# Loads of K and V in two row groups, and fewer stores in the last unit of an attention and mixer kernel

## The chip, the cores and the metric

The kernel runs on one core of a Trainium2 chip. The metric is the device time of one launch in microseconds (us). Five engines work side by side, each through its own queue in order: TensorE (PE: matmuls and transposes), VectorE (DVE), ScalarE (ACT), GpSimd (POOL) and SyncE (SP). Transfers between HBM and the on-chip memory run on 16 DMA engines. An engine issues a transfer as an instruction in its own queue; the data move later, and a semaphore tells of the landing.

## What is computed

Attention with pooled keys and values for 8 batches, 8 heads, 576 rows and 64 columns a head, then a token mixer and a channel mixer:

```python
k_p = k.reshape(B, H, Sp, 8, D).mean(axis=3)       # Sp = 576 / 8 = 72 pooled rows
v_p = v.reshape(B, H, Sp, 8, D).mean(axis=3)
scores = scale * np.matmul(q, k_p.transpose(0, 1, 3, 2))
attn = softmax(scores)                             # over the 72 pooled keys
x = heads_side_by_side(np.matmul(attn, v_p))       # 8 x 576 x 512
h = np.maximum(x.transpose(0, 2, 1) @ w_tok1, 0) @ w_tok2
u = x + h.transpose(0, 2, 1)
out = u + np.maximum(u @ w_ch1, 0) @ w_ch2         # w_ch1 512 x 1536
```

## The kernel before

Everything is one launch on one core, with the order of the work written out by hand: each engine executes its instructions in the order in which the program names them.

**Units.** The channel mixer is done in nine units. Units 0 to 7 are batches 0 to 7 with 512 of their 576 rows; unit 8 holds the last 64 rows of all batches together (the tails). A unit multiplies `u` with `w_ch1` on PE (L473), applies ReLU on ACT (L477) and multiplies with `w_ch2` (L496 in unit 0, L545 from unit 1 on, where the product is computed with sums of operands that VectorE prepares, L514 to L534).

**Schedule tables.** A unit is a generator with some 48 stops. At each stop, tables (L23 to L39) name the attention and token steps of later batches that are put in there. `K0`, `K1`, `V0`, `V1` pool half the heads of a batch's keys or values on POOL (L170, L171, L174 or L176), `k1` and `v1` the same on VectorE. `kpT` transposes the pooled keys on PE (L219) and copies them on VectorE (L221). `Q0`, `Q1` transpose queries on VectorE (L268), `s0` to `s3` are scores (PE L279, exponentials on ACT L285), `av` is the product with the values (PE L317, division on VectorE L335), `at`, `u` and `t` the token mixer (L363, L378, L388). `lk`, `lq`, `lv` issue the loads of a later batch's K, Q and V. A prefix gives the batch: `<` this unit's own, none the next, `>` the one after. `g` is a gate: VectorE sets a flag (L630) and POOL copies it (L631), so that POOL's next instructions start no earlier than that point of VectorE's order.

**Loads.** All loads of K, Q, V and weights are issued by POOL, since they cast from float32 to bfloat16. K and V of a batch are 72 pooled rows on 72 partitions, 8 heads and 8 rows of 64 each. Batch 0's are loaded in three parts (64 rows of four heads, the last 8 rows of all heads, 64 rows of the other four heads), those of batches 1 to 7 in one transfer of 576 KB. Each of the tiles `kr`, `vr` and `qb` has two buffers. Ahead of unit 0, POOL's order is (L660 to L682): K, Q, V of batch 0 (transfers 1 to 7), token weights (8 to 12), first channel weights (13 to 15), K of batch 1, a permutation of weights, Q and V of batch 1, second channel weights in three, then K and Q of batch 2. In unit 0 the step `lv2` stands at stop 10 and `K0` of batch 1 at stop 15, so POOL issues the load of batch 2's V ahead of that pooling; `lk3` at stop 16 and `V0` at 18 follow.

**Swap.** From batch 4 on, `u` is written to HBM (`mem`, L397) and read back in blocks (`v<-mem`, L404), both issued by SP, and transposed in blocks by VectorE (L411) into what the next unit's PE work reads.

**Stores.** A unit's output goes out from tiles of 128 partitions: two tiles of two 128-row groups (`oa` and `ob`, 512 columns each). `store` (L480) issues two transfers a tile from SP, one for each half of 64 partitions, because a group of 128 partitions holds rows of two kinds. In unit 8 the groups are the tails of two batches each; `oa` goes out with `store`, and `ob` in eight transfers (L572 to L581): for each column half, each of the two groups and each half of the partitions one, alternately on SP and ACT, as soon as the addition for that group is done.

Of the kernel before, what the change touches and what calls it, by code (L numbers as in the profile page):

```python
# [19 lines left out]

HEAD = """c0 c1 d8 q0 d1 q1 d5 kp0 kp1 kt0 d2 o0 e0 kt1 kp2 kp3 o1 e1 kt2 kt3 q2 q3 d2 o2 e2 vpool0 o3 d1 vpool1 e3 d2
          aw1 av0 av2 d2 av3 at_0 at_2 av4 at_1 at_3 d2 at_4 X0 X1 X2 A0 A1 A2 X3 A3 d3"""
FIRST = {0: "<u0", 2: "<u3", 6: "k1", 10: "lv2", 15: "K0 Q0", 16: "kpT Q1 lk3", 18: "V0 s1 <u2", 20: "s0",  # L23
         22: "lq3 v1 s2", 24: ">K0 s3", 25: "av1", 26: "av4", 27: "<u1 av3 av2", 30: ">K1", 32: "av0", 36: "at0 at1",
         38: "u3 >V0", 40: "u4 u0", 44: "lv3 u2 u1", 45: "t3 t0", 46: "t1", 47: "t2 t4"}
SECOND = {4: "g0", 7: ">K0 kpT", 8: "Q1", 9: "Q0", 11: "s2", 12: ">Q0", 13: ">Q1", 14: "v1 =3a s0", 15: "lv3 lk3",
          16: "s1", 17: "=1a", 18: "s3 =3b", 19: "av1", 20: "av3", 21: "av2", 22: "lq3", 23: ">K1 av0", 24: "av4",
          26: "g1", 27: "=1b", 28: ">kpT =2a", 29: "at0", 30: ">s3", 31: "=2b", 32: "=4b at1 =4a", 34: ">s2",
          36: "u2", 38: ">V0", 39: "u0 >s1 u3", 40: "t2", 41: "u1 t3", 42: ">s0 >V1 t0 t1"}
THIRD = {0: ">K0 av4 lk3 lq3", 2: "av3", 4: ">K1", 6: "av0", 9: "av2", 10: ">V0 av1", 12: "=3b", 14: "at0 at1",  # L30
         15: "=3a", 16: ">kpT", 17: "g0", 18: ">Q0", 19: "=1a u3 >s1", 20: ">Q1", 23: "u1 >s3 =2a", 24: "u0 =1b u2",
         25: "=2b t1", 26: ">s0", 28: "u4 >s2 =4b", 29: ">V1", 30: "=4a g1", 33: "t0", 34: "t2 >av3", 35: "t3",
         37: ">av4", 39: "t4 >av1", 41: "lv3", 42: ">av2", 44: ">av0"}
LATER = {0: ">Q0", 6: "=3a >K0", 7: "at0 at1", 8: ">K1 >kpT", 9: ">V0 u1 u0 >Q1", 10: "u3 >s1", 11: ">V1 u4",
         12: "u2", 13: ">s0", 14: "M0", 15: "M4 M2", 16: "M", 17: ">s3 lk3", 18: "=3b", 20: "=1a", 21: "g0",
         22: ">av3 =2a", 23: "=1b", 24: "lq3", 25: "=2b", 27: ">s2 =4a", 28: "=4b", 31: "g1 >av2", 36: ">av4",
         38: "T1 T3", 39: "T2", 40: "T0", 43: ">av0", 44: ">av1 lv3 T4"}
LAST = {14: "=3b", 22: "=1a", 24: "=2a =1b", 25: "=4a", 28: "=2b", 31: "=4b", 34: "=3a"}
PLANS = {0: FIRST, 1: SECOND, 2: THIRD, 8: LAST}  # L39


@with_exitstack
def kernel(
# [14 lines left out]
    nc = tc.nc  # L58
    B, H, S, D = q.shape
# [54 lines left out]
    def load_kv(b, src, key):  # L114
        t = loaded[b, key] = raw.tile([SP, H, POOL, D], BF16, name=key + "r")
        if b == 0:
            for h0, h1, j0, j1 in ((0, HP, 0, BP), (0, H, BP, SP), (HP, H, 0, BP)):
                kv(t, src, b, h0, h1, j0, j1)
        else:
            kv(t, src, b, 0, H)  # L120

    def load_q(b):
        qb = loaded[b, "q"] = raw.tile([P, HP, BR * D + D], BF16, name="qb")
# [9 lines left out]
    def load(key, b):  # L133
        if b < B:
            load_q(b) if key == "q" else load_kv(b, k if key == "k" else v, key)
# [334 lines left out]
    def l1_tile(n, m, uT):  # L470
# [6 lines left out]
        nc.scalar.activation(out=GT[:, m, :], in_=ps, func=AF.Relu)  # L477
        yield

    def store(n, g, o):  # L480
        for half in range(2):
            rows = slice(half * BP, (half + 1) * BP)
            if n == B:
                dst = out.rearrange("(c h) (p r) n -> h p c r n", h=2, r=BR)[half][:, 2 * g:2 * g + 2, 8, :]
            else:
                dst = out[n].rearrange("(p r) n -> p r n", r=BR)[:, 4 * g + half:4 * g + half + 3:2, :]
            nc.sync.dma_start(out=dst, in_=o[rows])

    def unit_plain(n, u):
# [46 lines left out]
    def unit_fast(n, u):  # L536
        last = n == B
        uT = moving(u)
        for m in range(NM):
            yield from l1_tile(n, m, uT)  # L540

        def product(ps, a, w, start, after, split=False):
            for i in range(2):
                for m in range(NH):
                    nc.tensor.matmul(out=ps[i] if split else ps[:, i], lhsT=a(m)[:, i * P:(i + 1) * P], rhs=w(m),  # L545
                                     start=start and m == 0 and (i == 0 or split), stop=(m == NH - 1),
                                     skip_group_check=True)
                    if (i * NH + m) % 4 == 3 and (i, m) != (1, NH - 1):
                        yield
                if split:  # L550
                    after(i)
            if not split:
                after(slice(0, 2))
            yield

        def bank(split=False):
            if split:
                return [ps_two.tile([P, 2, 512], FP32, name="p2")[:, 0, 0:256] for _ in range(2)]
            return ps_one.tile([P, 2, 256], FP32, name="p1")

        def keep(name):
            return outp.tile([P, 2, 256], FP32, name=name, bufs=1)

        def plus(out, ps, other, then=None):
            def go(i):
                nc.vector.tensor_tensor(out=out[:, i], in0=ps[i] if type(ps) is list else ps[:, i], in1=other[:, i],  # L566
                                        op=ALU.add)
                if then is not None:
                    then(i)
            return go  # L570

        def store_part(cols):  # L572
            def go(i):
                if not last:
                    return
                c = 2 + i
                for half in range(2):
                    (nc.scalar if half else nc.sync).dma_start(
                        out=out[2 * c + half].rearrange("(p r) n -> p r n", r=BR)[:, 8, cols],
                        in_=ob[half * BP:(half + 1) * BP, i, cols])  # L580
            return go  # L581

        SG, TW = fast["S"], fast["T"]
        u1, u2 = u["u"][:, 0:2], u["u"][:, 2:4]
        oa, ob = (outp.tile([P, 2, DM], FP32, name="o") for _ in range(2))
        x, y = bank(last), bank()
        s1 = keep("s1")
        yield from product(x, lambda m: GT[:, m, lo], lambda m: w_ch2[:, m, lo], True,
                           plus(s1, x, u1[:, :, lo]), last)
        yield from product(y, lambda m: GT[:, NH + m, lo], lambda m: w_ch2[:, NH + m, lo], True, plus(oa[:, :, lo], y, s1))  # L590
        z = bank()
        s5 = keep("s5")
        yield from product(z, lambda m: SG[:, 0, m], lambda m: TW[:, 0, m], True, plus(s5, z, u2[:, :, hi]))
        s2 = keep("s1")
        yield from product(x, lambda m: SG[:, 1, m], lambda m: TW[:, 1, m], False,
                           plus(s2, x, u1[:, :, hi]), last)
        if not last:
            w = bank()
            s4 = keep("s4")
            yield from product(w, lambda m: GT[:, NH + m, hi], lambda m: TW[:, 3, m], True, plus(s4, w, u2[:, :, lo]))  # L600
        yield from product(z, lambda m: SG[:, 3, m], lambda m: w_ch2[:, NH + m, hi], False, plus(oa[:, :, hi], z, s2))
        store(n, 0, oa)
        if last:
            yield from product(x, lambda m: SG[:, 2, m], lambda m: TW[:, 2, m], False,
                               plus(ob[:, :, hi], x, s5, store_part(hi)), True)
            yield from product(x, lambda m: GT[:, NH + m, hi], lambda m: TW[:, 3, m], False,
                               plus(ob[:, :, lo], x, u2[:, :, lo], store_part(lo)), True)
        else:
            def finish(i):
                plus(ob[:, :, hi], x, s5)(i)  # L610
                plus(ob[:, :, lo], x, s4)(i)
            yield from product(x, lambda m: SG[:, 2, m], lambda m: TW[:, 2, m], False, finish)
            store(n, 1, ob)
# [19 lines left out]
    def unit(n, at):  # L633
# [8 lines left out]
        for i, _ in enumerate((unit_fast if n >= 1 else unit_plain)(n, st)):  # L642
            for s in at.get(i, "").split():
                if s[0] == "=":
                    g_sums(s[1:])
                    continue
                if s[0] == "l":
                    load(s[1], n + int(s[2]))
                    continue
                if s[0] == "g":  # L650
                    gate()
                    continue
                ahead = {"<": 0, ">": 2}.get(s[0], 1)
                s = s.lstrip("<>")
                if n + ahead < B and ((n + ahead) % 2 or s not in ("u4", "t4", "M4", "T4")):
                    batches[n + ahead][1][s]()

    with tc.manual_schedule(engines={PE, POOLE, DVE, ACT, SYNC}):
        batches = [batch_steps(b) for b in range(B)]
# [21 lines left out]
        load("q", 2)  # L681
        batches[1][0]()  # L682
        for n in range(B + 1):
            unit(n, PLANS.get(n, LATER))


# [28 lines left out]
```

## Time and profile before

| | |
|---|---|
| time, median of 3 runs | 280.29 us (277.67 to 281.28) |
| span of the profiled execution, first to last instruction | 276.3 us; the page has no other time of this execution |
| PE, DVE, POOL, ACT busy | 261.1, 193.0, 144.8, 113.6 us |
| K and V loads of 576 KB, median from issue to landing | 11.0 and 8.7 us |
| POOL idle, waiting for VectorE's flag | 81.7 us in 14 waits |
| granted TensorE clock, mean | 0.995 |

The span is the time from the first to the last instruction of the program on the core; the time of a run also has what lies around it. A line of the timeline gives start, duration, engine, line of the kernel, operation, output<-input and count, and in brackets how long the engine was idle before it and what ended that. A line of the chain of waits gives start, duration and what the end of the run hung on at that time. A line of the waits gives who waited for whom, total us, times, and the longest. A line of the windows gives the stretch, its length, busy us of PE, weight loads, DVE, ACT and POOL with counts, the granted clock, the share of the DMA engines and GB/s.

### The profile page before, as it was taken

To read this page: it belongs to the slowest core of one execution; us is meant where nothing else is said; L and a number is where in the kernel's file an instruction comes from. 1 tells how busy PE (TensorE), PEld (TensorE's weight loads), DVE (VectorE), ACT (ScalarE), POOL (GpSimd) and SP (SyncE) were. 2 spreads that over 40 slices of the span, in tenths; PEclk is the share of its full clock that TensorE was granted. 3 is DMA by queue.
4 is the path that set the end of the run, shared out by engine and by line. 5 is a ranking of instruction groups with operands and counts; after the bars stand their busy time and mean duration, and the time that the engine had idled before them with its cause. 6 is when DMAs were issued, how large, how long until landed. Compare 5 with 4: busy or idle time off the path is not lost.

```text
span 276.3 us, 5208 instructions
## 1 busy us (share of the span) xinstructions
PE 261.1 (95%) x2064; PEld 156.1 (57%) x2092; DVE 193.0 (70%) x378; ACT 113.6 (41%) x200; POOL 144.8 (52%) x138
## 2 busy tenths in 40 slices
PE   7889889989999999999998999999999999999991
PEld 2765334444466654784486437843784486485581
DVE  5465987389999879897487857775794667263281
ACT  2453671107723456305920574057406412603600
POOL 8594793975989986299629962996000000000000
PEclk9999999999999999999999999999999999999997
DMA  7999999937590690074497549952305253204006
GB/s 161 193 202 206 205 205 186 202 68 152 76 168 14 118 203 4 6 114 123 109 171 131 155 108 170 169 154 80 76 2 152 97 96 79 77 0 132 23 0 152
DMA packets 36455, 32.71 MB, mean 118 GB/s; under 512 B 13776, under 2 KB 30032, under 8 KB 36432
## 3 DMA queue, kind: packets, MB, share of 16 engines
q0 software_dynamic: 18672, 17.64, 41.7%
q1 hardware_dynamic: 17440, 14.49, 20.7%
q8 instruction: 16, 0.26, 0.4%
q10 hardware_dynamic: 320, 0.26, 0.3%
q14 instruction: 7, 0.06, 0.1%
HBM read 38.21 MB, written 11.80 MB: 181 GB/s over the span
## 4 chain that ended last, share of the span: by engine, by line
PE 58%; DMA 17%; DVE 14%; POOL 4%; issue 2%; ACT 2%; SPq 2%; DVEq 0%; POOLq 0%; ACTq 0%
PE p L473 23%; PE p L545 18%; DMA v<-mem 8%; PE p L378 5%; DMA kr<-in_k_dram 5%; PE p L363 5%; DVE area L516 4%; DMA area<-in_moe_w_tok_dram 3%; PE p L496 3%; PE p L317 2%; PE p L279 2%; DMA mem<-u 2%; SPq L404 2%; DVE u L379 1%; DVE x L335 1%
## 5 line engine op out<-in xcount | busy, mean ns | idle before, releaser
L477 ACT ACTIVATE GT<-p 128x512 bf16<-128x512 f32 x108 | 64.4, 596 | 97.9 <-PE p L473 58.1
L473 PE MATMUL p<-uT,w_ch 128*128 128x512 bf16 x366 | 91.8, 383 | 2.7 <-DVE uT L411 1.1
L473 PEld LDWEIGHTS <-w_ch 128*128 128x128 bf16 x432 | 39.4, 97 | 48.8 <-issue 5.8
L631 POOL COPY flag<-flag 1x1 f32<-1x1 f32 x14 | 3.5, 247 | 81.7 <-DVE flag L630 81.7
L285 ACT ACTIVATE ex<-p 72x576 bf16<-72x576 f32 x56 | 33.1, 642 | 18.0 <-PE p L279 17.9
L545 PEld LDWEIGHTS <-area 128*128 128x128 bf16 x384 | 36.6, 98 | 5.1 <-issue 0.5
L545 PE MATMUL p<-area,area 128*128 128x256 bf16 x288 | 36.2, 273 | 0.0
L171 POOL TENSOR_TENSOR t<-t 72x512 f32<-72x512 f32 x25 | 34.3, 1372 | 2.0
L379 DVE TENSOR_TENSOR u<-p,x 128x512 bf16<-128x512 f32 x32 | 21.5, 684 | 13.5 <-PE p L378 13.3
L545 PEld LDWEIGHTS <-GT 128*128 128x128 bf16 x288 | 27.1, 98 | 6.2 <-issue 1.4
L170 POOL TENSOR_TENSOR t<-kr 72x1024 f32<-72x1024 bf16 x13 | 27.7, 2130 | 4.8 <-DMA kr<-in_k_dram 4.3
L170 POOL TENSOR_TENSOR t<-vr 72x1024 f32<-72x1024 bf16 x12 | 25.7, 2143 | 0.7
L545 PE MATMUL p<-w_ch,GT 128*128 128x256 bf16 x192 | 23.8, 273 | 0.1
L566 DVE TENSOR_TENSOR o<-p,s 128x512 f32<-128x512 f32 (+1 forms) x32 | 20.6, 663 | 2.6 <-PE p L545 2.6
L523 DVE TENSOR_TENSOR area<-GT 128x768 bf16<-128x768 bf16 x16 | 10.3, 642 | 16.8 <-ACT GT L477 16.7
L335 DVE TENSOR_TENSOR x<-p,den 128x512 bf16<-128x512 f32 x30 | 20.7, 691 | 1.0
L566 DVE TENSOR_TENSOR s<-p,u 128x512 f32<-128x512 f32 x28 | 19.2, 685 | 3.2 <-PE p L545 3.1
L516 DVE TENSOR_TENSOR area<-GT 128x768 bf16<-128x768 bf16 x16 | 13.5, 849 | 9.6 <-ACT GT L477 9.6
L317 PEld LDWEIGHTS <-ex 72*128 72x128 bf16 x320 | 14.9, 98 | 7.1 <-DVE x L335 1.3
L378 PE MATMUL p<-AT,w_tok 128*128 128x512 bf16 x63 | 17.8, 379 | 0.4 <-DVE u L379 0.4
L317 PE MATMUL p<-vp,ex 72*128 72x65 bf16 x320 | 16.8, 194 | 1.1 <-DVE x L335 0.3
L354 ACT ACTIVATE AT<-p 128x512 bf16<-128x512 f32 x15 | 9.0, 597 | 20.8 <-PE p L363 18.1
(102 smaller groups left out, 322.9 us busy)
## 6 DMA issues: line engine op xcount, KB each, us to landing
out_dram<-o SPq DMA_DIRECT2D x34, 256.0 KB, 3.5
kr<-in_k_dram POOLq DMA_DIRECT2D x7, 576.0 KB, 11.0
qb<-in_q_dram POOLq DMA_DIRECT2D x7, 576.0 KB, 12.4
vr<-in_v_dram POOLq DMA_DIRECT2D x7, 576.0 KB, 8.7
w_ch<-in_moe_w_ch_dram POOLq DMA_DIRECT2D x6, 512.0 KB, 13.5
mem<-u SPq DMA_DIRECT2D x8, 256.0 KB, 2.1
v<-mem SPq DMA_DIRECT2D x8, 160.0 KB, 6.7
v<-mem SPq DMA_DIRECT2D x8, 128.0 KB, 5.3
```

The source lines that it names most:

```text
L170: eng.tensor_tensor(out=t4[:, 0:n], in0=t[:, hs, 0:4], in1=t[:, hs, 4:8], op=ALU.add)
L171: eng.tensor_tensor(out=t4[:, 0:n, 0:2], in0=t4[:, 0:n, 0:2], in1=t4[:, 0:n, 2:4], op=ALU.add)
L285: nc.scalar.activation(out=exv[:, h:h + 2], in_=pss[a][0:SP, :, 0:SH], func=AF.Exp, scale=scale)
L317: nc.tensor.matmul(out=halves[h // 4][:, (h % 4) * (D + 1):(h % 4 + 1) * (D + 1)], lhsT=st["ex"][:, h * S + n0:h * S + n0 + P], rhs=st["vp ...
L335: nc.vector.tensor_tensor(out=dst.rearrange("p (a h d) -> p a h d", a=2, d=D), in0=view[:, :, :, 0:D], in1=den[rows, :, :, None].broadcast ...
L378: nc.tensor.matmul(out=ps, lhsT=w, rhs=a, start=(i == 0), stop=(i == len(mms) - 1))
L379: nc.vector.tensor_tensor(out=dst, in0=ps, in1=x, op=ALU.add)
L473: nc.tensor.matmul(out=ps, lhsT=w_ch1[:, kk, m * P:(m + 1) * P], rhs=uT[kk], start=(kk == 0), stop=(kk == 3))
L477: nc.scalar.activation(out=GT[:, m, :], in_=ps, func=AF.Relu)
L516: nc.vector.tensor_tensor(out=out, in0=a, in1=b, op=ALU.subtract)
L545: nc.tensor.matmul(out=ps[i] if split else ps[:, i], lhsT=a(m)[:, i * P:(i + 1) * P], rhs=w(m), start=start and m == 0 and (i == 0 or spli ...
L566: nc.vector.tensor_tensor(out=out[:, i], in0=ps[i] if type(ps) is list else ps[:, i], in1=other[:, i], op=ALU.add)
```

## The change

Each K and V load of batches 1 to 7 is issued as two transfers, one of 64 rows and one of 8 rows (`BP` is 64, `SP` 72). In the last unit, `oa` is stored in one transfer of 128 partitions, and each column half of `ob` in one transfer of 128 partitions and both groups, issued when the second group's addition is done: the first half by ACT, the second by SP. The schedule tables are written in another notation, one for each unit with batch numbers spelled out; expanded, old and new name the same steps at the same stops in the same order.

```diff
-PLANS = {0: FIRST, 1: SECOND, 2: THIRD, 8: LAST}
+PLAN = [
+    {0: "0.u0", 2: "0.u3", 6: "1.k1", 10: "2.lv", 15: "1.K0 1.Q0", 16: "1.kpT 1.Q1 3.lk", 18: "1.V0 1.s1 0.u2", ...
...
         else:
-            kv(t, src, b, 0, H)
+            kv(t, src, b, 0, H, 0, BP)
+            kv(t, src, b, 0, H, BP, SP)
...
+    def tail_rows(g, cols):
+        rows = out.rearrange("b s n -> (b s) n").rearrange("(c p r) n -> p c r n", p=P, r=BR)
+        return rows[:, 2 * g:2 * g + 2, 8, cols]
+
     def store(n, g, o):
+        if n == B:
+            nc.sync.dma_start(out=tail_rows(g, slice(0, DM)), in_=o)
+            return
         for half in range(2):
             rows = slice(half * BP, (half + 1) * BP)
-            if n == B:
-                dst = out.rearrange("(c h) (p r) n -> h p c r n", h=2, r=BR)[half][:, 2 * g:2 * g + 2, 8, :]
-            else:
-                dst = out[n].rearrange("(p r) n -> p r n", r=BR)[:, 4 * g + half:4 * g + half + 3:2, :]
+            dst = out[n].rearrange("(p r) n -> p r n", r=BR)[:, 4 * g + half:4 * g + half + 3:2, :]
             nc.sync.dma_start(out=dst, in_=o[rows])
...
-        def store_part(cols):
+        def store_part(cols, engine):
             def go(i):
-                if not last:
-                    return
-                c = 2 + i
-                for half in range(2):
-                    (nc.scalar if half else nc.sync).dma_start(
-                        out=out[2 * c + half].rearrange("(p r) n -> p r n", r=BR)[:, 8, cols],
-                        in_=ob[half * BP:(half + 1) * BP, i, cols])
+                if i == 1:
+                    engine.dma_start(out=tail_rows(1, cols), in_=ob[:, :, cols])
             return go
...
-                               plus(ob[:, :, hi], x, s5, store_part(hi)), True)
+                               plus(ob[:, :, hi], x, s5, store_part(hi, nc.scalar)), True)
...
-                               plus(ob[:, :, lo], x, u2[:, :, lo], store_part(lo)), True)
+                               plus(ob[:, :, lo], x, u2[:, :, lo], store_part(lo, nc.sync)), True)
```

## The prediction, made before the changed kernel ran

> **What bounds the kernel now.** First I read the page's busy times, then who TensorE (PE) waits for, then the chain of waits of the first 80 us, then POOL's timeline, and last the end of the run.
>
> ```profile
> PE 261.1 (95%) x2064; PEld 156.1 (57%) x2092; DVE 193.0 (70%) x378; ACT 113.6 (41%) x200; POOL 144.8 (52%) x138
> ```
>
> PE is busy 95% of the span, so a stall put into PE's order is hardly won back later, and an edit away from PE gains only where PE waits now. The waits of PE come to 7.3 us in all; the largest:
>
> ```profile
> PE p L219 <- POOL kp L174: 1.6, 1, 1.6
> ```
>
> This is batch 1's transpose of pooled keys, held by POOL. The chain shows why POOL was late:
>
> ```profile
> 14.97 13.77 DMA kr<-in_k_dram
> 28.73 0.02 issue
> 28.77 0.56 issue
> 29.34 0.85 POOL vr L111
> 30.20 2.14 POOL t L170
> ...
> 35.05 0.30 PE p L219 x4
> ```
>
> POOL pools batch 1's keys (K0) only at 30.20, because ahead of it in its queue stands the load of batch 2's V, and that issue waited until batch 1's K had landed (28.73). The two share no buffer. POOL's timeline shows what the rule is:
>
> ```profile
> 11.07 0.52 POOL L146 DMA_DIRECT2D w_tok<-in_moe_w_tok_dram  x1 [1.02 <-DMA qb<-in_q_dram]
> 12.29 2.25 POOL L159 DMA_DIRECT2D w_ch<-in_moe_w_ch_dram  x3 [0.70 <-DMA vr<-in_v_dram]
> 14.97 0.86 POOL L111 DMA_DIRECT2D kr<-in_k_dram  x1 [0.43 <-DMA area<-in_moe_w_tok_dram]
> ...
> 25.09 0.71 POOL L128 DMA_DIRECT2D qb<-in_q_dram  x1 [1.61 <-PE p L435]
> ...
> 29.34 0.85 POOL L111 DMA_DIRECT2D vr<-in_v_dram  x1 [3.54 <-PE p L473]
> ```
>
> Number POOL's transfers in order of issue. The row at 11.07 is the 12th; the 4th was issued at 3.83 and landed 7.0 later, at 10.8. The 13th (12.29) follows the landing of the 5th (4.56 + 7.4 = 12.0), the 16th (14.97) that of the 8th (14.68, in the chain), the 23rd (25.09) that of the 15th (13.79 + 10.7 = 24.5), the 24th (29.34) that of the 16th (28.73). Five of five: a POOL transfer is issued only when the one eight before it has landed. Where the row names PE, PE was only the last releaser by the profile.
>
> **The head: eight transfers, now smaller.** The change turns each K and V load of batches 1 to 7 into two transfers, so eight places hold fewer bytes. Counting again: batch 1's K is 16 and 17, its Q 18, its V 19 and 20, the second channel weights 21 to 23, batch 2's K 24 and 25, its Q 26, its V 27 and 28. So batch 2's V now waits for batch 1's **V** (19, 20), where it waited for batch 1's K. Behind it on POOL stand K0 of batch 1, batch 3's K load and V0; PE waits for K0.
>
> Batch 1's V was issued at 19.49 and landed 14.6 later, at 34.0. The transfers are saturated there (0.9 busy or more from 14 to 50 us) and the bytes are the same, so the last 8 rows land between 33.4 and 34.9. The early end: the 8-row pieces of K and V fall on different engines, and the busiest is spared one row, 8 packets of 78 ns (512 packets of channel weights, 32 an engine, take the 2.5 us from the 14th landing, 13.05 + 9.0, to the 15th). The late end: the 8 rows land 0.9 after the whole did, as the 8-row piece of batch 0 (2.06 + 5.4 = 7.5) landed 0.9 after the piece before it (1.25 + 5.3 = 6.6). I take 33.8, nearer to where equal bytes land. Then 0.6 us to the issue (28.73 to 29.34) and 0.61 for an 8-row issue (row of batch 0): K0 starts at 35.0, or 35.1 if the 64-row issue is what comes last. It took 4.79 us beside VectorE's own pooling (30.20 to 34.99); alone POOL takes 4.36 (46.31 to 50.67). VectorE will be done with its half by then, so keys are ready at 39.5 and PE resumes at 39.55 instead of 35.05: **+4.5** (4.0 to 5.7). POOL itself makes this up: it sat idle 4.3 us before 46.31. PE has nothing to do meanwhile, the next instructions in its order being this transpose.
>
> A page of the Trainium skill would give less. DMA: Bandwidth & Descriptors, section "Why a DMA increments its semaphore by 16 and not by 1", says a transfer uses the largest number of engines up to 16 that divides its rows, which is 12 for 72, with an exception of 16 engines with rows rounded up. By the 12, each K and V load would fall from 6 rows on its busiest engine to 5, V would land 1.3 us sooner and this term be +3.2, the sum 4.3. The trace decides for the exception, by the first line here:
>
> ```profile
> 118.50:121.50 3.00, 3.00 (x47) 2.77 (x44) 2.93 (x9) 0.00 (x0) 2.77 (x4) 1.00 0.90 150
> ...
> 270.00:273.50 3.50, 0.58 (x6) 0.27 (x3) 0.81 (x2) 0.00 (x0) 0.00 (x0) 1.00 0.94 237
> 273.50:276.20 2.70, 0.00 (x0) 0.00 (x0) 0.00 (x0) 0.00 (x0) 0.00 (x0) 0.50 0.32 76
> ```
>
> The last columns are granted clock, share of the 16 transfer engines and GB/s. In 118.5 to 121.5 one 72-row load (batch 5's V) runs alone, and the share is 0.90, more than 14 engines. 72 rows on 15 engines are 5 on the busiest; 64 rows are 4, and the 8 add one on 8 engines: 5 again. A single load gains nothing.
>
> **The clock.** PE would stand idle from 33.47 to 39.5, 6 us. The other two lines show what idling does: the last matmuls end at 270.6 (269.11 + 1.47), and from 273.5 on the granted clock is 0.5. PE's timeline shows what a start costs: the first eight 512-column matmuls took 3.20 us, soon after five took 1.24 and three 0.81, a step of 0.215, by which eight take 1.9. The start lost 1.3. After a stall of 6 us I expect the same: 1.3, or twice that, 2.6, if low speed lasts twice as long, or 0 if the clock holds. I take **+1.5**, next to the row that exists.
>
> **Fourteen more issues on POOL.** A 72-row issue takes 0.85, an 8-row one 0.61, a 64-row one between 0.64 (half the heads) and 0.85: each split adds 0.4 to 0.6. Nearly everywhere POOL's waits for VectorE's flag (81.7 us in total) cover that. One place is tight: in unit 1 POOL ends batch 3's keys at 77.19 and PE transposes them at 77.61, 0.42 later, and between the flag at 65.06 and this end stand the loads of batch 4's V and K. Two splits add 1.2, less 0.42: **+0.8** (0 to 1.3). VectorE's copy of these keys follows at 78.12, and the chain runs through VectorE there, so it counts. For batches 4 to 7 the same distance is 3 to 5 us and one split falls into it: 0.
>
> **Units 3 and 4.** The swap through memory (v<-mem, 10.9 and 10.1 us in the chain) shares engines with the K and Q loads. PE waits 1.1 us for it in all. The bytes on the busiest engine are equal, so I put 0; below, the whole 1.1 could go, above, an 8-row piece queued ahead could add its 0.9 in each unit.
>
> **The last stores.** VectorE ends at 271.03. Behind it:
>
> ```profile
> 270.04 3.71 SPq L578 DMA_DIRECT2D out_dram<-o  x4
> 270.61 0.42 DVE L566 TENSOR_TENSOR o<-p,u_tails 128x256 f32<-128x256 f32 x1 [0.23 <-PE p L545]
> ```
>
> SP's issues back up: the last begins at 273.2 and lands 2.1 later, at 275.3. Merged, it begins at 271.1, with 256 KB in place of 64. The nearest rows are the spills, 256 KB from 128 partitions in 1 KB pieces, 2.1 us to landing; the slowest store of 256 KB near the end took 3.9. That gives 273.2 to 275.0. Also, 1 MB in all has to go out from about 269.9 (1.2 after the first issue at 268.69), and at the 237 GB/s of the window line that lasts to 274.3. I take 274.1: **-1.2** (-2.0 to -0.2). The first merged store has twice the bytes, and nothing waits for it but the end.
>
> The rewritten schedule table lists the same steps at the same places: 0.
>
> **Sum**: 4.5 + 1.5 + 0.8 - 1.2 = +5.6 on the profiled span of 276.3. The profile gives no time of its own beside the span; the median of the runs, 280.29, is 4.0 above it (runs from 277.67 to 281.28). Start-up and end are not touched, so 280.3 + 5.6 = **285.9**.
>
> **Rivals.**
> - *The clock stays low.* After the stall PE meets a stretch that ScalarE's exponentials set (38.43 to 42.28 in the chain), and PE may pause often enough that full clock returns only past 45. Then 3 us more are lost: 288.9. For it: full speed came at the start after gapless work. Against it: PE is busy 6.75 of the 7 us from 35 to 42. Chance 0.15.
> - *Not slower.* Batch 2's V does not hold POOL: its two pieces go out before 31 (the rule of eight doesn't hold for them, or batch 1's V lands as early as its K). Then K0 starts as before or earlier, PE's 1.6 us wait may go, the end gives 1.2: 277.5 to 279.9, about 278.6. For it: issues 1 to 11 show too few waits to test the rule. Against: the five that fit. Over 2% faster would need 5.6, and all gains together give 4.7 (1.6, the 1.1 of the swap, 2.0 at the end); the runs of before spread by 3.6, so I leave part of it there. Chance 0.13, of it 0.06 faster.
> - *The clock doesn't drop*, or the head costs 3.2 by the 12-engine rule: 284.4 or 284.6, within the forecast's own range.
>
> **Numbers.** Forecast 0.68, its own range 283 to 288; the bound of 2%, about what a measurement of this kernel can tell from no change, is 5.6 us, the middle of it: 0.36 slower, 0.32 same. The low-clock rival adds 0.15 slower; the other 0.07 same, 0.06 faster; the 0.04 left is same. In all 0.06, 0.43, 0.51. The range that leaves out no more than 2 in 10 reaches from 279.5, which cuts half the not-slower case, to 289.
>
> **What would show it.** Right: POOL's issues of batch 2's V start after 33, K0 of batch 1 near 35, PE's wait at L219 is about 6 us, granted clock under 1 near 38 to 43, L219 in unit 1 waits 0.8, and only two or three stores after 268 with the last landing near 4 us after VectorE's last addition at most. Wrong: K0 at 30 as before; then the head term and the clock fall away together and the end's gain is what is left.

## The result, and the profile after

The changed kernel takes 282.31 us (median of 20 runs, 280.86 to 283.69) against 279.32 for the kernel before in the same series (20 runs, 277.67 to 281.61). The ratio is 1.009, 95% interval 1.0065 to 1.0116: slower by about 2.5 us (3.0 between the medians), where 5.6 was forecast. The ratios here and below leave out runs over 1.5% above the fastest of the same kernel; six of twelve runs of one kernel below (b6on_lv2_late), its profiled run among them, fall out by that, so its ratio speaks for the other half alone. The profiled execution of the changed kernel spans 280.7 us (its run: 282.52), 4.4 more than the one of before. Lines of the kernel are numbered five or six lower up to a unit's first products, for instance L105 for the K and V loads, L165 to L171 for POOL's pooling, L214 for the keys' transpose, and one lower in its second products (L544).

First the page's busy times of the changed kernel, then PE's longest wait, then its chain of waits in the first 60 us:

```profile
PE 264.1 (94%) x2064; PEld 157.4 (56%) x2092; DVE 191.2 (68%) x378; ACT 113.6 (40%) x200; POOL 150.6 (54%) x152
```

```profile
PE p L214 <- POOL kp L169: 6.2, 2, 5.9
```

```profile
19.04 13.81 DMA vr<-in_v_dram
32.90 0.50 issue
33.40 1.27 POOL vr L105 x2
34.69 2.14 POOL t L165
...
39.11 0.42 PE p L214 x4
```

The keys' transpose waits 5.9 us in place of 1.6. The chain ahead of it now runs through the landing of batch 1's **V** (32.9), which batch 2's V issue waits for; K0 starts at 34.69 instead of 30.20. POOL's timeline of the changed kernel shows each of the issues waiting for the one eight before it:

```profile
24.22 0.74 POOL L158 DMA_DIRECT2D w_ch<-in_moe_w_ch_dram  x1 [1.76 <-DMA w_ch<-in_moe_w_ch_dram]
27.46 1.28 POOL L105 DMA_DIRECT2D kr<-in_k_dram  x2 [2.50 <-PE p L373]
29.91 0.72 POOL L123 DMA_DIRECT2D qb<-in_q_dram  x1 [1.17 <-DMA qb<-in_q_dram]
33.40 1.27 POOL L105 DMA_DIRECT2D vr<-in_v_dram  x2 [2.76 <-DMA vr<-in_v_dram]
```

POOL is held four times there, 8.2 us in all. Where a row names PE, PE was only the last releaser by the profile. The windows of the same stretch (granted clock third from the right; the share of the transfer engines next to it adds up the packets' times, and since packets of one engine overlap it can pass 1) show what the stall does to PE:

```profile
30.00:37.10 7.10, 3.21 (x15) 1.27 (x13) 0.89 (x2) 2.39 (x4) 4.24 (x5) 1.00 1.24 204
37.10:43.90 6.80, 4.43 (x20) 1.58 (x22) 2.02 (x4) 1.96 (x4) 6.54 (x7) 0.50 1.21 209
43.90:50.00 6.10, 5.90 (x55) 2.30 (x55) 5.42 (x5) 4.81 (x9) 5.92 (x5) 1.00 1.23 203
```

The clock is at half for 6.8 us, and 4.8 of these lie after PE has resumed at 39.11. At the end of the run, from the timeline:

```profile
275.83 0.41 ACTq L574 DMA_DIRECT2D out_dram<-o  x1
...
276.70 0.42 DVE L565 TENSOR_TENSOR o<-p,u_tails 128x256 f32<-128x256 f32 x1 [0.23 <-PE p L544]
277.15 0.40 SPq L574 DMA_DIRECT2D out_dram<-o  x1
```

The last store is issued 0.03 after VectorE's last addition and takes 0.40 to issue. From that addition to the end of the span are 3.6 us, where it was 5.2.

Setting VectorE's instructions of the two executions side by side gives the shift at each place: +4.2 at the copy of batch 1's keys, +6.3 when the products with the values begin, +6.6 after batch 3's keys, +5.1 after the swap of unit 3, +5.7 at batch 6's keys, +6.1 from the swap of unit 4 to the last addition, and +4.4 at the end.

### The profile page after: what moved, and what is told of

Read it like the earlier page. It is cut to its first block, busy times and chain, and to the rows that moved or that the text cites. A ratio compares the mean times of both kernels' runs of the same rounds, so it can differ in the third digit from the quotient of the medians.

```text
span 280.7 us, 5212 instructions
## 1 busy us (share of the span) xinstructions
PE 264.1 (94%) x2064; PEld 157.4 (56%) x2092; DVE 191.2 (68%) x378; ACT 113.6 (40%) x200; POOL 150.6 (54%) x152
## 4 chain that ended last, share of the span: by engine, by line
PE 64%; DVE 13%; DMA 12%; POOL 5%; issue 3%; ACT 2%; SPq 1%; DVEq 0%; POOLq 0%; ACTq 0%
PE p L468 24%; PE p L544 21%; DMA vr<-in_v_dram 7%; PE p L373 5%; PE p L358 5%; DMA v<-mem 4%; DVE area L515 4%; PE p L495 3%; PE p L312 2%; PE p L274 2%; DVE x L330 1%; DVE qD L263 1%; DVE u L374 1%; POOL kr L105 1%; ACT ex L280 1%
## 5 line engine op out<-in xcount | busy, mean ns | idle before, releaser
L468 PE MATMUL p<-uT,w_ch 128*128 128x512 bf16 x366 | 93.1, 387 | 2.3 <-DVE uT L406 0.8
L544 PEld LDWEIGHTS <-area 128*128 128x128 bf16 x384 | 36.6, 98 | 5.1 <-issue 0.5
L544 PE MATMUL p<-area,area 128*128 128x256 bf16 x288 | 36.2, 273 | 0.0
L166 POOL TENSOR_TENSOR t<-t 72x512 f32<-72x512 f32 x25 | 33.0, 1319 | 2.0
L544 PEld LDWEIGHTS <-GT 128*128 128x128 bf16 x288 | 27.1, 98 | 6.2 <-issue 1.4
L165 POOL TENSOR_TENSOR t<-kr 72x1024 f32<-72x1024 bf16 x13 | 27.7, 2133 | 0.5
L165 POOL TENSOR_TENSOR t<-vr 72x1024 f32<-72x1024 bf16 x12 | 25.9, 2159 | 0.7
L544 PE MATMUL p<-w_ch,GT 128*128 128x256 bf16 x192 | 23.8, 273 | 0.1
```

The source lines that it names most:

```text
L165: eng.tensor_tensor(out=t4[:, 0:n], in0=t[:, hs, 0:4], in1=t[:, hs, 4:8], op=ALU.add)
L166: eng.tensor_tensor(out=t4[:, 0:n, 0:2], in0=t4[:, 0:n, 0:2], in1=t4[:, 0:n, 2:4], op=ALU.add)
L468: nc.tensor.matmul(out=ps, lhsT=w_ch1[:, kk, m * P:(m + 1) * P], rhs=uT[kk], start=(kk == 0), stop=(kk == 3))
```

## The experiments

The theory: a POOL transfer waits for the one eight places before it; splitting makes eight places short; POOL, then PE, stall; PE's clock halves. Rivals: the pieces cost by themselves; the loss after the stall is not the clock. Twelve runs, each timed in turns with the kernel before.

### The parts alone

tail_only has the loads of before (`kv(t, src, b, 0, H)`), split_only the ten stores of before.

> The last unit's three stores alone, K and V loads whole as before. The two profiles say that the end (VectorE's last addition to the end of the span) fell from 5.3 to 3.6 us, so: end 3.6, head as before (K0 of batch 1 on POOL near 30, PE's wait at the keys' transpose 1 to 2 us, granted clock 1.0 throughout), time 279.3 - 1.7 = 277.6, ratio 0.994. Rival, the end's gain belongs to the shifted phase and not to the stores: end 5 us, ratio 1.000.

> The split loads alone, ten stores at the end as before. If parts add up: PE's wait near 6 us, half clock for 7 us, end 5.3 us, time 282.3 + 1.7 = 284.0, ratio 1.017. Rival, the split's cost shown by the two profiles is partly the run's own spread: ratio near 1.010 or less.

Measured: 0.9934 (0.9905 to 0.9962) for the stores alone, with 3.2 us at the end and the clock at 1.0; 1.0186 (1.0146 to 1.0225) for the loads alone, with 5.6 us at the end and PE's wait at 5.4. The stores give 1.8 us, the split loads cost 5.2. Both ratios are near what was expected. The half clock in split_only's profile lasts 3.4 us, though, and not the 7 expected. Added up, the two parts give 1.012, and the changed kernel has 1.009; the intervals cover that difference.

### Moving one step past the wait: lv2_late

```diff
-10: "2.lv", 15: "1.K0 1.Q0"
+15: "1.K0 2.lv 1.Q0"
```

> The changed kernel with one step moved: the load of batch 2's V is issued behind the pooling of batch 1's keys (K0) instead of ahead of it; loads stay split, nothing is left out. Theory of eight places: POOL is held by batch 2's V until batch 1's V lands, so K0 now starts right behind batch 2's Q issue (near 30.7 instead of 34.7), PE waits 1.5 to 2 us instead of 5.9, the clock stays at 1.0, and 4.1 + 2.2 us come back: 276 to 277, ratio 0.988 to 0.992. Rival, the pieces cost by themselves (14 more issues on POOL, later landings): the time stays at 280 or more, ratio 1.003 or above.

Measured: 0.9967 (0.9935 to 0.9999), 278.1 us. 3.4 us come back, not 6.3; the ratio is above the 0.988 to 0.992 expected and below the rival's 1.003. From POOL's timeline:

```profile
30.93 2.13 POOL L165 TENSOR_TENSOR t<-kr 72x1024 f32<-72x1024 bf16 x1
...
38.19 0.57 POOL L105 DMA_DIRECT2D kr<-in_k_dram  x1 [0.96 <-DMA w_ch<-in_moe_w_ch_dram]
38.78 2.13 POOL L165 TENSOR_TENSOR t<-vr 72x1024 f32<-72x1024 bf16 x1
```

K0 starts at 30.93, as the theory says. But the rule of eight meets the next load, too: the second piece of batch 3's K waits for the second channel weights (37.91 in the chain), and V0 behind it ends late, at 44.3; the products with the values are then held by V0, and the chain of waits runs through it. PE's wait at the keys is still 2.1, and the clock falls for 3.4 us.

### The clock: warm

```diff
-16: "1.kpT 1.Q1 3.lk"
+16: "d24 1.kpT 1.Q1 3.lk"
```

`d24` is 24 matmuls on a zeroed tile, as the head of the kernel uses them.

> The changed kernel with 24 matmuls of zeros, whose result nobody reads, ahead of batch 1's key transpose on PE, about 5.2 us at full clock inside a stall of 5.9. Clock theory: the stall's end does not move (K0 starts at 34.7 as before), but the clock stays at 1.0, and the 2.2 us that VectorE's additions lost between the transpose and the products with the values come back: 280.1, ratio 1.002 to 1.004. Rival, those 2.2 us come from the order of the work after the stall (ScalarE's exponentials, queries' transposes), not from the clock: 282.3, ratio 1.009.

Measured: 1.0024 (0.9992 to 1.0056), 279.8 us. From the windows of this run:

```profile
39.00:46.00 7.00, 6.87 (x56) 2.48 (x56) 5.72 (x6) 5.82 (x11) 6.82 (x7) 1.00 1.19 207
```

K0 starts at 34.6 and the transpose at 39.1, as in the changed kernel; the clock stays at 1.0, and 1.8 us are gone (ratio 0.0066 lower). PE's order is the same otherwise, so the clock is the cause of that part. With some 1.1 us either way, the 1.8 is clear of noise, its exact size is not.

### Places or bytes: split_b2

```diff
-            kv(t, src, b, 0, H, 0, BP)
-            kv(t, src, b, 0, H, BP, SP)
+            if b == 2:
+                kv(t, src, b, 0, H, 0, BP)
+                kv(t, src, b, 0, H, BP, SP)
+            else:
+                kv(t, src, b, 0, H)
```

> Only batch 2's K and V are split, all other loads whole, the end as changed. Theory of eight places: the counting makes batch 2's second V piece the 26th transfer, which waits for the 18th, batch 1's whole V (near 33.5). So K0 starts at 34.3 to 35.3 although every load ahead of it is as before, PE waits 5 to 6 us, the clock falls to half; +5 for head and clock less 1.8 at the end: 282.0 to 283.0, ratio 1.008 to 1.013. Rival, the size of the landing transfers or the issue time of the pieces delays K0: two more issues of 0.6 us, K0 near 31, ratio 0.995 to 0.998.

POOL's timeline in this run:

```profile
31.84 0.71 POOL L105 DMA_DIRECT2D vr<-in_v_dram  x1 [1.47 <-DMA qb<-in_q_dram]
34.26 0.59 POOL L105 DMA_DIRECT2D vr<-in_v_dram  x1 [1.71 <-DMA vr<-in_v_dram]
34.86 2.13 POOL L168 TENSOR_TENSOR t<-kr 72x1024 f32<-72x1024 bf16 x1
```

The 25th transfer waits for the 17th (Q), the 26th for the 18th (V), and K0 starts at 34.86. Batch 2's own K, ahead of it, is split too (the expectation overlooks that), but the two loads that are waited for, the 17th and the 18th, are whole as before. The rule counts transfers, not bytes: this is shown. The time, though, is 1.0177 (1.0125 to 1.023), above the 1.013 expected. In the profiled run, where the loads of batches 6 and 7 are whole, PE waits 2.6 us for the swap of unit 4, and the clock falls there for another 3.4 us. That second fall does not explain the ratio: the profiled run has a mean clock of 0.979, the two other runs behind the ratio have 0.985, near the changed kernel's 0.986, and are as slow (284.1 and 284.4 us). But it pointed to units 3 and 4.

### Whole loads beside the swap

split_b6on splits batches 6 and 7 alone (`b >= 6`), with the three stores; whole_lv2_late has whole loads, the stores and batch 2's V behind K0; b6on_lv2_late is both.

> Split only in batches 6 and 7, whose loads run beside the swap in units 3 and 4; head and unit 1 as in the run with the three stores alone (ratio 0.9934). Theory that the split relieves the swap: PE's waits for the swapped blocks come to 0.3 to 1.2 us as in the four profiles with split loads (0.77, 0.59, under 0.5, 1.18) and not 1.1 to 2.6 as in the two with whole loads; 1 us, ratio 0.988 to 0.992. Rival, the swap's wait is scatter from one execution to the next: ratio 0.9925 to 0.996.

> All loads whole, three stores at the end, and batch 2's V issued behind K0. K0 then starts when batch 1's K lands (28 to 28.8) and ends near 33.5, where PE arrives: PE's wait 0 to 0.4 us in place of 1.6 and 0.6, and no execution has the half clock there (before: 7 of 29 with a mean clock of 0.990 or less). 279.3 - 1.8 - 1.0 - 0.5 = 276.0, ratio 0.988. Rival, K0 is held by its own keys' landing and VectorE's work on them, and nothing moves: 0.9934 as with the stores alone.

> The last two together: three stores, batch 2's V behind K0, K and V of batches 6 and 7 split. If the split relieves the swap: 1 us below the run without it, near 275.0, ratio 0.984. Rival: the same as without it, 0.988.

Measured: 0.9899 (0.9864 to 0.9934), 0.9882 (0.9849 to 0.9914) and 0.9864 (0.9829 to 0.9898). Each interval lies below 1. The split of 6 and 7 alone gives 0.0035 over the stores, 1.0 us with some 1.3 either way, the moved V 0.0052, both inside the intervals, and the third kernel's profile, of a run that its ratio leaves out, has a wait of 3.8 us in unit 4 in spite of the split. One of the six runs of whole_lv2_late has a mean clock of 0.985, so the expectation that none would lose the clock there failed. This does not settle whether the split relieves the swap.

The next two undo that part of the changed kernel: split_upto5 loads 6 and 7 whole (`b < 6` splits), even_b6on cuts them in 36 and 36 rows.

> The changed kernel with the loads of batches 6 and 7 whole again; head, unit 1 and end as in the changed kernel. If the split of these two relieves the swap (profiles so far: PE's waits in units 3 and 4 come to 1.1, 2.6, 1.8 and 2.7 us with whole loads there, to 0.8, 0.6, 0.4, 1.2, 0.6 and once 3.8 with split ones), the time rises by about 1 us over the changed kernel: ratio 1.011 to 1.014. Rival, the waits scatter whatever the loads are: 1.009.

> The changed kernel with K and V of batches 6 and 7 cut in 36 and 36 rows instead of 64 and 8. If two smaller transfers in place of one are what relieves the swap, the time is that of the changed kernel: ratio 1.007 to 1.012, K of batches 6 and 7 landed about 7 us after its first issue. If the 64 rows are (four on each of 16 engines), the relief goes, as with whole loads there: K lands after 8 us or more, ratio 1.016 to 1.022.

Measured: 1.0206 (1.0156 to 1.0256) and 1.0200 (1.0145 to 1.0254), against 1.009 (1.0065 to 1.0116) with 64 and 8 rows. Undoing it costs 0.0116, 3.2 us with some 1.6 either way (2.2 between the plain medians), more than the 1 us expected, and the even cut costs as much: two smaller transfers alone do nothing, the cut at 64 does. That is the case in which the 64 rows bring the relief, as even_b6on's expectation has it. PE's wait for the swapped blocks, in the changed kernel, in split_upto5 and in even_b6on:

```profile
PE p L468 <- DVE uT L406: 0.8, 1, 0.8
```

```profile
PE p L471 <- DVE uT L409: 1.8, 2, 1.6
```

```profile
PE p L469 <- DVE uT L407: 2.4, 2, 2.3
```

And batch 6's K from issue to landing, from the transfers' view cut to its issue, whole in the kernel before and in two pieces in the changed one:

```profile
kr<-in_k_dram POOLq DMA_DIRECT2D x1, 576.0 KB, 8.2
```

```profile
kr<-in_k_dram POOLq DMA_DIRECT2D x1, 512.0 KB, 6.3
```

```profile
kr<-in_k_dram POOLq DMA_DIRECT2D x1, 64.0 KB, 6.3
```

The second piece is issued 0.7 after the first, so all 72 rows are there 7.0 us after the first issue, 1.2 sooner. In split_upto5 the whole load takes 8.1, and in even_b6on the second piece lands 7.9 after its own issue, 8.6 after the first. The slowest transfer of the swap takes 10.9 us in the changed kernel, 11.7 in split_upto5 and 12.3 in even_b6on.

The side-by-side of VectorE's instructions places only a part of the 3.2 us. From batch 3's keys to the last addition, which takes in units 3 and 4, the kernels with whole loads of batches 6 and 7 took longer than the profiled execution of before, by 1.5 (tail_only), 3.0 (split_b2), 0.6 (whole_lv2_late) and 0.7 us (split_upto5), and even_b6on by 1.3. With 64 and 8 rows beside the swap they took less, by 0.5 (the changed kernel), 0.7 (split_only), 1.4 (lv2_late), 0.1 (warm) and 0.7 us (split_b6on), and once 4.1 more (b6on_lv2_late). So split_upto5 lost 1.2 us there against the changed kernel, and another 1.2 ahead of it, where the two kernels do the same work; that part is scatter between two executions.

### Taking the loads out of the swap's way: early_loads, early_split

On top of whole_lv2_late, `6.lk 6.lq` go behind `5.K0` in unit 3 and `7.lk 7.lq` behind `6.K0` in unit 4, from stops 17 and 24. early_split has batches 6 and 7 split as well.

> The kernel with whole loads, three stores and batch 2's V behind K0 (ratio 0.988), with one more move: K and Q of batches 6 and 7 are issued right behind the pooling of half the keys of batches 5 and 6, so that they land before the swap begins. Theory that the swap shares the engines with these loads: its four transfers land in 5 to 7 us as in unit 5, where no load runs (4.6), instead of 10 to 16; PE waits for no swapped block, no execution loses the clock there, and 1 to 2 us come back: ratio 0.980 to 0.985. Rival, the swap is slow by itself in units 3 and 4, or the moved issues hold up POOL's pooling of the next batch: 0.988 or more.

> The kernel with early loads (ratio 0.983) with the split of K and V in batches 6 and 7 put back. If the split's only worth is that loads beside the swap land sooner, it is worth nothing once they are out of its way: ratio 0.981 to 0.986, PE waits for no swapped block in either. Rival, split loads are cheaper in themselves: 0.975 or less.

Measured: 0.9833 (0.9772 to 0.9893), 274.45 us, the fastest of all, and 0.9858 (0.9803 to 0.9913). The swap's transfers in early_loads:

```profile
DMA to landing us min/median/max: 2.5/3.3/5.0
```

The slowest takes 5.0 us, where the changed kernel has 10.9; PE waits for no swapped block in either run. With the loads away from the swap the split brings nothing that can be seen; 0.0025 lies between the two, with 0.008 or 2.3 us either way, so a worth of 1 us would not show. This agrees with a worth that lay in the swap and does not prove it. The early loads themselves give 0.0049 over whole_lv2_late, also inside the intervals.

## Why the prediction was right or wrong

**Head: right.** Batch 2's V waits for batch 1's V; issue at 33.40, K0 at 34.69, PE at 39.11: +4.1 where 4.5 was forecast; split_b2 confirms the counting. Some luck is in the size. Batch 1's V landed at 32.9, 0.9 before the 33.8 taken and ahead of the whole range given (33.4 to 34.9); half of that is its issue at 19.04 in place of 19.49. Against it, both pieces of batch 2's V were issued after that landing, in 1.27 us, and not the last one alone (0.61).

**Clock: right in kind, a little low.** Half speed for 6.8 us; warm measures 1.8, forecast 1.5. In the two profiles, shift from 4.2 to 6.3, it is 2.1. The low-clock rival's further 3 us did not come: full clock was back at 43.9.

**POOL's issues ahead of batch 3's keys: right place, too large.** PE's wait there is 0.3 and the shift grows by 0.3, from 6.3 to 6.6; forecast 0.8.

**Together** these three made 6.8 in the forecast and 6.6 in the two profiles. split_upto5 and tail_only differ only in the splits of batches 1 to 5, where all three lie; the ratios are 0.0272 or 7.6 us apart, with some 1.6 either way. With batches 6 and 7 split, the same step is from split_b6on to the changed kernel: 0.0191 or 5.3 us, with some 1.2 either way.

**The last stores: too small.** 1.8 against 1.2. The last landing came 2.2 after its issue, the spill's row, which was one end of the range; the bound from 237 GB/s did not bind.

**Units 3 and 4: the step that failed.** "The bytes on the busiest engine are equal, so I put 0; below, the whole 1.1 could go." Measured: -3.2 us, with some 1.6 either way (split_upto5 against the changed kernel), of which the two profiles place 1.2 there. Two things were wrong in it.

The first is the count of engines. The prediction read a share of 0.90 as more than 14 of the 16 engines, so that 72 rows put 5 on the busiest, as 64 and 8 do. But the share adds up overlapping packets. Where all transfers of the kernel before run together it is 1.19, at 210 GB/s:

```profile
24.60:28.70 4.10, 4.10 (x21) 1.86 (x19) 1.86 (x8) 1.78 (x3) 0.71 (x1) 1.00 1.19 210
```

Against this, 0.90 and 150 GB/s are 0.76 and 0.71 of the full rate, near 12 engines of 16. The packet records of the trace say it directly: of the 427 packets of 1 KB that start from 118.4 to 121.4, when batch 5's V is loaded alone, 422 fall into twelve rows in which one starts about every 79 ns; each takes some 98 ns, hence the overlap. In the changed kernel, when the 64 rows of the same load are under way (125.25 to 126.25), the share is 1.24, at 193 GB/s. So, as an estimate, a whole load puts 6 rows on its busiest engine, and a load in 64 and 8 rows 5. That the busiest engine is spared a row fits K's landing 1.2 us sooner, and two cuts of 36, if they run on 12 engines each, spare it none. DMA: Bandwidth & Descriptors of the Trainium skill, section "Why a DMA increments its semaphore by 16 and not by 1", has the rule that the prediction set aside, by which 72 rows go to 12 engines, 36 rows to 12 and 64 rows to all 16. The trace agrees for 72 rows; a load of 36 rows alone is in no trace here. How K's sooner landing turns into less waiting for the swap is argued from the landings and not isolated by a run.

The second is the floor of 1.1: it was one execution's wait. The other profiles with whole loads in batches 6 and 7, the even cut counted with them, show 2.6, 2.6, 1.8, 1.8 and 2.4 us; those with 64 and 8 rows beside the swap 0.8, 0.6, under 0.5, 1.2, 0.6 and once 3.8. So the profiled execution of before was at the low end of its kind there; that other executions of the same kernel lose more is inferred from these kernels. The longest single waits, 2.6 us in split_b2 and 3.8 in b6on_lv2_late, came with another 3.4 us of half clock; 2.3 in even_b6on did not.

This is a part of why the profiles differ by 4.4 us and the ratio says 2.5. Among 29 runs of before in the first series of experiments, 7 have a mean granted clock of 0.990 or less and 280.7 us on average; the other 22 average 279.0, the mean of all is 279.4. All 20 runs of the changed kernel are at 0.990 or less. The profiled execution of before was among the undisturbed ones, and a fast one of these: with the 1.8 us that lie between span and time in the changed kernel's profiled run it took some 278.1, an estimate. No kept trace shows a slower run of before, so where those lose their time is not shown.

**The sum.** 7.6 - 1.8 - 3.2 = +2.6 is the ratio taken apart (the steps run from before over tail_only and split_upto5 to the changed kernel), so that it comes out confirms nothing. Taken the other way, over split_b6on, the same change is 5.3 - 1.8 - 1.0. In both, units 3 and 4 give back time for which the forecast had 0; how much of the missing 3.1 us is theirs (3.2 or 1.0), and whether the terms of the head were too small or too large, stays open within these intervals. In the two profiles alone, forecast and measurement are +6.8 and +6.6 for the three terms of the head and unit 1, 0 and -0.5 for units 3 and 4, and -1.2 and -1.6 for the end.

The rival in which the change ends not slower fell: its condition, batch 2's V issued before 31, did not hold. The one with a head of 3.2 rested on the 12 engines, which the trace bears out, but the head came to 4.1.

## What to carry to other kernels

Count an engine's transfers as well as their bytes: where an issue waits for the one a fixed number of places back, cutting loads in pieces moves every later issue nearer to a landing, and what stands behind it in the queue pays. Put loads behind the work that the next engine waits for, and out of the way of a transfer that sets the pace: here both moves together took the kernel with the three stores from 0.9934 to 0.9833, 2.8 us, about what the whole change cost. Compare a share of the transfer engines with its value where they are saturated before reading engines off it: 0.90 was 12 engines here, not 14. A wait seen in one execution is no floor for what an edit can save, where runs of the kernel scatter by more than that wait.

## What the runs showed that was not expected

A store from all 128 partitions takes 0.40 us to issue whether it has 512 KB (at 274.78 in the changed kernel) or 256; one from 64 partitions takes 0.60 alone and up to 1.4 in the queue of ten. Stretches of half clock between PE's first and last work last 3.4 or 6.8 us in every profile that has one; this agrees with TensorE: Matmul & The Clock Gate of the Trainium skill, Part 1, which gives a window of about 3.4 us. And a 72-row load beside the swap is better cut at 64 than in halves, in the changed kernel by 0.011 of the run's time.
